# Fused attention, gated MLP and product MLP on one core: a third buffer for the down products' high parts, prepared weights stored in 1 KB runs, and attention's PSUM banks closed apart from its stores

## The chip, the core and the metric

One core of a Trainium2 chip runs the whole program in one launch. The metric is the device time in microseconds (us), the median of several runs. TensorE is called PE here, VectorE DVE, ScalarE ACT, GpSimd POOL, and SyncE SP; all large transfers are issued in order from SP's queue. PE's clock has two levels, 2.4 and 1.2 GHz; a granted clock of 1.00 is the upper one.

## The reference

```python
def _attn_ref(q, k, v, tau):                 # q, k, v: (4, 8, 576, 64), tau: 0.02
    scores = scale * np.matmul(q, k.transpose(0, 1, 3, 2))
    thresh = np.max(scores, axis=-1, keepdims=True) - tau
    scores = np.where(scores >= thresh, scores, -1000000000.0)
    attn = np.exp(scores - np.max(scores, axis=-1, keepdims=True))
    attn = attn / (np.sum(attn, axis=-1, keepdims=True) + 1e-09)
    return np.matmul(attn, v).astype(np.float32)
def _moe_ref(x, w_in, w_out):                # x: (2304, 512), w_in: (512, 2048)
    h = x @ w_in
    return ((h * (1.0 / (1.0 + np.exp(-h)))) @ w_out).astype(np.float32)
def _moe2_ref(x, w_a, w_b, w_out):           # w_a, w_b: (512, 1536)
    return ((x @ w_a) * (x @ w_b) @ w_out).astype(np.float32)
```

The attention's output goes through the gated MLP (MLP1) and then through the product MLP (MLP2). The weights come as float64.

## The kernel before

**The work.** Attention runs as 144 tiles of 128 query rows by 576 keys. A tile is scored on PE (L512, L519), DVE takes the row minimum of the negated scores (L528), ACT the exponential (L542), DVE masks and sums (L545), PE transposes the result (L577) and multiplies it by v (L622). MLP1 takes the tokens in five blocks of 256 and two of 512 (blocks 5 and 6), each in 16 units of 128 hidden columns: ups into bank hb or hc (L747), tanh on ACT (L757), the gate on DVE (L760), a rounded high part on ACT (L763) and the low part on DVE (L766), then downs into the y banks (L807). Every product is three fp32r matmuls: high by low, high by high, low by high. MLP2 takes the tokens in three tiles of 768 and works by a Strassen-Winograd scheme with seven products (`ORDER`): per tile six groups of up products (L1120, 504 matmuls of 384 columns), then the down products (L1206, 252 matmuls). The sums between products are chain() on DVE and ACT (p1, u2, v, c22, c21, c12: L1048 to L1065).

**Weights.** MLP1's 32 chunks (split_weight) are rebuilt from float64 words during the early attention: low word and scaled high word on ACT, sign (L354) and join (L359) on DVE, the integer sum (total, L363) in four POOL pieces, high part on ACT (L367), low part on DVE (L371). Two raw buffers (wraw), one wc buffer. MLP2's 36 units (split_unit) are rebuilt during MLP1's last blocks and stored to DRAM (L905) in seven combinations each, from which MLP2 streams 512 KB tiles (L960).

**Order.** Nothing is placed by hand. Class Plan simulates the engines with costs in nanoseconds and issues the task of lowest rank that is ready; buffers are rings (RINGS), and a task that takes a ring's buffer waits for its release. The resulting order per engine is then fixed, since each engine issues in order; semaphores do the waiting at run time. The costs of a task, its rank and the ring sizes thus decide which instruction stands ahead of which. On SP, loads and stores share that one order.

**What the change touches.** RINGS: xr5 (raw x of blocks 5 and 6), tm (results of chain, 768 columns), zh (rounded high parts of the down products' inputs). split_weight and w1_chunk; load_x (low part of x, L719); split_unit and prepare_weights with dv() and ac(), the planner's costs; stream; the task `closed`, behind all of attention's tasks, at which the memory of attention is given back and the banks hc and y5 are opened:

```python
    closed = pl.add("none", 1, 0, close_attention, behind=[*att_tasks, *closed0])
    l = pl.add("DVE", dv(2 * n), rank, lo, [h], [lo_take])
    st = {x: dma(-1, P * 8 * TN, store(x, half, par), after=[s[t]])
```

The second line is the low part zl of a down product's input (its own ring has two buffers), the third the four stores of a down phase's results, which hold their tm buffers until they land.

## Time and profile before

| what | value |
|---|---|
| median of 3 runs | 1140.99 us (1138.83 to 1143.01) |
| profiled execution | 1144.45 us, span 1142.6 us |
| mean granted clock of PE | 0.987 |
| busy, share of the span | PE 97%, DVE 72%, ACT 50%, POOL 18% |
| attention with MLP1's first units | 0 to 490 us |
| rest of MLP1, preparation of MLP2's weights | 490 to 736 us |
| MLP2, three tiles | 736 to 1143 us |

The span is the time between the first and the last instruction on the core; the profiled execution's own time has 1.85 us around it. An engine's share is its busy time over the span, an average over stages that differ.

### The profile page before, as it was taken

The page shows a single profiled execution, that of the slowest core. Times are in us where ns is not written, and L with a number is a line of the kernel's source. Part 1 is how long each engine was busy: PE and PEld are TensorE (multiplying, and loading weights), DVE is VectorE, ACT ScalarE, POOL GpSimd, SP SyncE. Part 2 cuts the span into 40 slices and gives each one's busy share as a digit, 9 for nine tenths or more (in the row PEclk, how much of TensorE's full clock was granted, in tenths as well). Part 3 has the DMA queues.
Part 4 walks back from the last instruction along what each step waited for, and adds up shares of the span by engine and source line. Part 5 has one row for each costly group of instructions (what it writes and reads, how often), then busy time and mean ns, then how long its engine had stood idle before and what let it go on. Part 6 is the DMA issues. An engine that isn't in the chain of part 4 may idle for free.

```text
span 1142.6 us, 19524 instructions
## 1 busy us (share of the span) xinstructions
PE 1105.2 (97%) x7097; PEld 985.2 (86%) x7097; DVE 822.8 (72%) x1702; ACT 574.1 (50%) x1012; POOL 201.9 (18%) x386
## 2 busy tenths in 40 slices
PE   8889998999999999999999899999989999999998
PEld 6457766898889989999888688899989999999998
DVE  8888887777777777739888789566764668546664
ACT  7777776666766676646665645311332113411133
POOL 2445444333423343122000200000000000000000
PEclk9989999999999999999999899999999999999999
DMA  6554454222332232139999979988879878887882
GB/s 198 184 166 155 147 156 122 97 80 87 89 98 75 76 104 75 38 123 273 287 269 284 276 219 327 323 247 255 256 261 304 249 255 246 269 281 253 248 252 75
DMA packets 147231, 222.27 MB, mean 195 GB/s; under 512 B 8112, under 2 KB 107584, under 8 KB 147136
## 3 DMA queue, kind: packets, MB, share of 16 engines
q1 hardware_dynamic: 146992, 221.03, 62.4%
q8 instruction: 56, 0.92, 0.3%
q14 instruction: 39, 0.32, 0.1%
q10 hardware_dynamic: 144, 0.00, 0.0%
HBM read 173.74 MB, written 47.26 MB: 193 GB/s over the span
## 4 chain that ended last, share of the span: by engine, by line
PE 81%; DMA 7%; DVE 5%; ACT 4%; issue 2%; POOL 1%; SPq 0%; POOLq 0%; DVEq 0%; ACTq 0%
PE pr L1120 23%; PE hb L747 11%; PE pr L1206 9%; PE sb L807 8%; PE av L622 6%; PE tp L577 5%; PE hc L747 5%; PE sa L512 4%; PE yc L807 2%; PE yd L807 2%; PE ye L807 2%; PE yf L807 2%; DMA wraw<-w_out 1%; DMA xi<-r_d 1%; DMA wraw<-w_in 1%
## 5 line engine op out<-in xcount | busy, mean ns | idle before, releaser
L1120 PE MATMUL pr<-w 128*128 128x384 f32 x1512 | 262.6, 334 | 0.0
L1120 PEld LDWEIGHTS pr<-w 128*128 128x128 f32 x1512 | 262.2, 188 | 0.1
L747 PE MATMUL hb<-xh,w 128*128 128x256 f32 (+1 forms) x704 | 156.9, 312 | 2.6 <-DVE th L760 1.9
L528 DVE TENSOR_SCALAR_CACHE_REDUCE t<-sa,nscale 128x576 f32<-128x576 f32 x128 | 103.5, 809 | 53.0 <-PE sa L512 45.5
L1206 PE MATMUL pr<-zh,w 128*128 128x384 f32 x504 | 129.2, 338 | 0.0
L545 DVE SCALAR_TENSOR_TENSOR e<-t,thr,e 128x576 f32<-128x576 f32 x128 | 112.0, 876 | 23.8 <-ACT e L542 22.3
L747 PEld LDWEIGHTS hb<-xh,w 128*128 128x128 f32 x704 | 113.9, 191 | 12.8 <-DVE th L760 3.1
L577 PE MATMUL tp<-ident,e 128*128 128x128 f32 x706 | 107.5, 280 | 12.0 <-DVE e L545 7.5
L577 PEld LDWEIGHTS tp<-ident,e 128*128 128x128 f32 x706 | 79.7, 142 | 36.4 <-issue 14.2
L542 ACT ACTIVATE e<-t,min 128x576 f32<-128x576 f32 x128 | 99.8, 781 | 19.7 <-DVE t L528 18.7
L747 PE MATMUL hb<-xl,w 128*128 128x256 f32 (+1 forms) x352 | 107.1, 304 | 0.7 <-POOL xl L719 0.7
L807 PE MATMUL sb<-gh,w 128*128 128x256 f32 (+1 forms) x576 | 98.1, 301 | 0.0
L1206 PEld LDWEIGHTS pr<-zh,w 128*128 128x128 f32 x504 | 91.9, 190 | 0.0
L1206 PE MATMUL pr<-zl,w 128*128 128x384 f32 x252 | 86.4, 343 | 4.9 <-DVE zl L975 4.8
L807 PEld LDWEIGHTS sb<-gh,w 128*128 128x128 f32 x576 | 80.1, 190 | 6.3 <-issue 3.3
L971 ACT CAST zh<-z 128x768 fp32r<-128x768 f32 x45 | 37.5, 833 | 84.1 <-PE pr L1206 58.4
L363 POOL TENSOR_TENSOR wt<-wc,wt 128x128 uint32<-128x128 uint32 x128 | 62.3, 517 | 77.3 <-DVE wc L359 48.4
L1132 ACT COPY yo<-pr 128x384 f32<-128x384 f32 x18 | 8.7, 481 | 123.7 <-PE pr L1120 123.7
L747 PEld LDWEIGHTS hb<-xl,w 128*128 128x128 f32 x352 | 67.1, 191 | 3.7 <-POOL xl L719 0.9
L512 PE MATMUL sa<-sp 128*128 128x288 f32 (+1 forms) x400 | 69.9, 300 | 0.0
L584 ACT COPY pb<-tp 128x512 f32<-128x512 f32 (+2 forms) x128 | 60.3, 493 | 17.7 <-PE tp L577 17.5
L719 POOL TENSOR_TENSOR xl<-xr,xh 128x128 fp32r<-128x128 f32 x72 | 39.3, 574 | 165.5 <-ACT xh L716 160.9
(140 smaller groups left out, 2016.6 us busy)
## 6 DMA issues: line engine op xcount, KB each, us to landing
w<-wab_d SPq DMA_DIRECT2D x126, 512.0 KB
w<-wo_d SPq DMA_DIRECT2D x63, 512.0 KB
wab_d<-uw SPq DMA_DIRECT2D x18, 896.0 KB
qk<-qk SPq DMA_DIRECT2D x20, 576.0 KB
wo_d<-uw SPq DMA_DIRECT2D x10, 896.0 KB
wraw<-w_in SPq DMA_DIRECT2D x16, 512.0 KB
wraw<-w_out SPq DMA_DIRECT2D x16, 512.0 KB
v<-v SPq DMA_DIRECT2D x20, 320.0 KB
```

The source lines that it names most:

```text
L363: nc.gpsimd.tensor_tensor(out=s["t"][:, o], in0=s["c"][:, o].bitcast(U32), in1=s["t"][:, o], op=ALU.add)
L512: nc.tensor.matmul(s["s"][:r + m, j, :NH], lhsT=hd["t"][:, 0, c - r:c + m], rhs=hd["t"][:, k, j * NH:(j + 1) * NH], start=(k == 1), stop=( ...
L528: nc.vector.tensor_scalar(out=s["t"], in0=s["s"][:, :, :NH], scalar1=nscale, scalar2=None, op0=ALU.mult, op1=ALU.min, accum_out=s["min"])
L542: nc.scalar.activation(out=s["e"], in_=s["t"], func=AF.Exp, scale=-1.0, bias=s["min"])
L545: nc.vector.scalar_tensor_tensor(out=s["e"], in0=s["s"][:, :, :NH] if early else s["t"], scalar=s["thr"], in1=s["e"], op0=ALU.is_ge if ear ...
L577: nc.tensor.transpose(t["tp"][:, j * P:(j + 1) * P], e["e"][:, o:o + P], ident)
L584: nc.scalar.copy(out=dst(s["p"]), in_=t["tp"][:, :m * P] if m < 4 else t["tp"].rearrange("p (k q) -> p k q", k=4))
L622: nc.tensor.matmul(s["av"][h * D:(h + 1) * D, :nq], lhsT=v["v"][:, h, k], rhs=s["p"][:, k, h * nq:(h + 1) * nq], start=(k == 0), stop=(k = ...
L747: nc.tensor.matmul(s["h"], lhsT=w[:, a, o:o + P], rhs=xx, start=(c == 0 and k == 0), stop=(c == NC - 1 and k == 2))
L807: nc.tensor.matmul(ys[j][e // per][:, e % per * tn:(e % per + 1) * tn], lhsT=w[:, a, e * P:(e + 1) * P], rhs=gs[j, f][g], start=(f == 0 an ...
L1120: nc.tensor.matmul(bank[:, m, :TN], lhsT=w["w"][:, a, (2 * m + k) * P:(2 * m + k + 1) * P], rhs=y[i][x][:, k, :TN], start=(i in (1, 6, 5) ...
L1206: nc.tensor.matmul(bank[:, c, :TN], lhsT=w["w"][:, a, (2 * e + c) * P:(2 * e + c + 1) * P], rhs=z[x][:, e], start=(i in (1, 6, 5) and sl = ...
```

## The change

xr5 and zh get a third buffer, tm loses one of five. The integer sum of the MLP1 chunks of the last two column groups (16 of 32) goes from POOL to DVE. The low part of block 6's x goes from POOL to DVE. Prepared weights are laid out so that a unit's high and low rows lie side by side, in SBUF and in DRAM, and its store writes runs of 1 KB where it wrote 512 bytes. Planner costs change: fixed parts of dv() and ac(), the sign step, more bytes and slack for the prepared weights' transfers. Attention's PSUM pools get their own stack, closed by a task (closed_p) that stands behind attention's PE, ACT and DVE tasks only; closed still stands behind its stores.

```diff
-    wab_d = dram.tile([NG, 7, P, 2, 4, P], F32, name="wab_d")
+    wab_d = dram.tile([NG, 7, P, 4, 2, P], F32, name="wab_d")
...
-    p1, p1x, px, att, psb = (ExitStack() for _ in range(5))
-    RINGS = dict(qk=2, sp=2, v=1, t=2, e=4, pa=1, pb=1, sa=1, sb=1, tp=2, hb=1, hc=1, yc=1, yd=1, ye=1, yf=1, xr5=2, x5=5, g5=2, th5=1, av=1, x=1, xi=1, rs=1,
+    p1, p1x, px, att, attp, psb = (ExitStack() for _ in range(6))
+    RINGS = dict(qk=2, sp=2, v=1, t=2, e=4, pa=1, pb=1, sa=1, sb=1, tp=2, hb=1, hc=1, yc=1, yd=1, ye=1, yf=1, xr5=3, x5=5, g5=2, th5=1, av=1, x=1, xi=1, rs=1,
...
-                 ur=2, us=2, uw=2, vr=2, vs=2, vw=1, yr=1, pr=4, tm=5, a11=2, zh=2, zl=2, **{f"z{k}": 3 for k in range(5)})
+                 ur=2, us=2, uw=2, vr=2, vs=2, vw=1, yr=1, pr=4, tm=4, a11=2, zh=3, zl=2, **{f"z{k}": 3 for k in range(5)})
...
-    ps_s = pool(att, "ps_s", 1, space=PSUM)
-    ps_t = pool(att, "ps_t", 2, space=PSUM)
-    ps_av = pool(att, "ps_av", 1, space=PSUM)
+    ps_s = pool(attp, "ps_s", 1, space=PSUM)
+    ps_t = pool(attp, "ps_t", 2, space=PSUM)
+    ps_av = pool(attp, "ps_av", 1, space=PSUM)
...
-    def split_weight(key, src, rank, dst, after=(), lo_engine="Pool", scale_engine="DVE", most=512):
+    def split_weight(key, src, rank, dst, after=(), lo_engine="Pool", scale_engine="DVE", most=512, total_engine="Pool"):
...
-            nc.gpsimd.tensor_tensor(out=s["t"][:, o], in0=s["c"][:, o].bitcast(U32), in1=s["t"][:, o], op=ALU.add)
+            eng = nc.gpsimd if total_engine == "Pool" else nc.vector
+            eng.tensor_tensor(out=s["t"][:, o], in0=s["c"][:, o].bitcast(U32), in1=s["t"][:, o], op=ALU.add)
...
-        ts = on_pool(512, rank, total, [j, l], most)
+        if total_engine == "Pool":
+            ts = on_pool(512, rank, total, [j, l], most)
+        else:
+            ts = [pl.add("DVE", dve_ns(512), rank, lambda: total(slice(0, 512)), [j, l], port=True)]
...
-        engines = dict(scale_engine=SCALE_ON[i % len(SCALE_ON)], lo_engine=LO_ON[i % len(LO_ON)], most=PIECE)
+        engines = dict(scale_engine=SCALE_ON[i % len(SCALE_ON)], lo_engine=LO_ON[i % len(LO_ON)], most=PIECE, total_engine=("Pool", "DVE")[j > 1])
...
-            def lo(o):
-                nc.gpsimd.tensor_tensor(out=s["l", c][:, o], in0=s["r", c][:, o], in1=s["h", c][:, o].bitcast(F32), op=ALU.subtract)
+            def lo(o, eng=nc.gpsimd):
+                eng.tensor_tensor(out=s["l", c][:, o], in0=s["r", c][:, o], in1=s["h", c][:, o].bitcast(F32), op=ALU.subtract)
...
-            l = on_pool(tn, R_AUX, lo, [h], PIECE)[-1]
+            if j == len(BLOCKS) - 1:
+                l = pl.add("DVE", dve_ns(tn), R_AUX, lambda: lo(slice(0, tn), nc.vector), [h], port=True)
+            else:
+                l = on_pool(tn, R_AUX, lo, [h], PIECE)[-1]
...
-                       behind=[up_last[0], *([closed] if c == 0 and bank == "hc" else [])])
+                       behind=[up_last[0], *([closed_p] if c == 0 and bank == "hc" else [])])
...
-                       banks if f == 0 and k0 == 0 else [], behind=[down_last[0], *([closed] if j >= 4 and f == 0 else [])])
+                       banks if f == 0 and k0 == 0 else [], behind=[down_last[0], *([closed_p] if j >= 4 and f == 0 else [])])
...
-        return int(n / 0.96 + 170)
+        return int(n / 0.96 + 67)
...
-        return int(n / 1.2 + 180)
+        return int(n / 1.2 + 93)
...
-            s["w"] = new("w", [P, 2, 7, P], F32R)
-            nc.scalar.copy(out=s["w"][:, 0], in_=s["a"][:, 1:])
+            s["w"] = new("w", [P, 7, 2, P], F32R)
+            nc.scalar.copy(out=s["w"][:, :, 0], in_=s["a"][:, 1:])
...
-            eng.tensor_tensor(out=s["w"][:, 1], in0=s["a"][:, 1:], in1=s["w"][:, 0].bitcast(F32), op=ALU.subtract)
+            eng.tensor_tensor(out=s["w"][:, :, 1], in0=s["a"][:, 1:], in1=s["w"][:, :, 0].bitcast(F32), op=ALU.subtract)
...
-            nc.sync.dma_start(out=dst.rearrange("i p l n -> p l i n"), in_=s["w"].bitcast(F32))
...
-        a = dma(rank, P * 4096, load, n=2, take=[lane + "r"], behind=behind)
+            nc.sync.dma_start(out=dst.rearrange("i p l n -> p i l n"), in_=s["w"].bitcast(F32))
...
+        a = dma(rank, P * 4096 * 6 // 5, load, n=2, slack=SLACK, take=[lane + "r"], behind=behind)
...
-        h = pl.add("DVE", 600, rank, sign, [a, c], port=True)
+        h = pl.add("DVE", 335, rank, sign, [a, c], port=True)
...
-        st = dma(rank, P * 7168, store, after=[o], slack=SLACK)
+        st = dma(rank, P * 7168 * 6 // 5, store, after=[o], slack=SLACK)
...
-                    units.append(((m, k, g), [r[h, k, :, :, g * P:(g + 1) * P] for h in range(2)], wab_d[g, :, :, :, 2 * m + k]))
+                    units.append(((m, k, g), [r[h, k, :, :, g * P:(g + 1) * P] for h in range(2)], wab_d[g, :, :, 2 * m + k]))
...
-                units.append((("o", g, c), [r[h, g, :, :, c * P:(c + 1) * P] for h in range(2)], wo_d[:, g // 2, :, :, g % 2, c]))
+                units.append((("o", g, c), [r[h, g, :, :, c * P:(c + 1) * P] for h in range(2)], wo_d[:, g // 2, :, g % 2, c]))
...
-            s["w"] = pools["ws"].tile([P, 2, 512], F32R, name="w")
-            nc.sync.dma_start(out=s["w"].bitcast(F32), in_=src)
+            s["w"] = pools["ws"].tile([P, 2, 512], F32R, name="w").rearrange("p a (q l n) -> p (a q) l n", q=2, l=2)
+            nc.sync.dma_start(out=s["w"].rearrange("p q l n -> p q (l n)").bitcast(F32), in_=src)
...
-            w = stream(wab_d[g, PART[i]].rearrange("p l q n -> p l (q n)"),
+            w = stream(wab_d[g, PART[i]].rearrange("p q l n -> p q (l n)"),
...
-                            nc.tensor.matmul(bank[:, m, :TN], lhsT=w["w"][:, a, (2 * m + k) * P:(2 * m + k + 1) * P],
+                            nc.tensor.matmul(bank[:, m, :TN], lhsT=w["w"][:, 2 * m + k, a],
...
-                w = stream(wo_d[PART[i], sl].rearrange("p l g c n -> p l (g c n)"),
+                w = stream(wo_d[PART[i], sl].rearrange("p g c l n -> p (g c) (l n)"),
...
-                                nc.tensor.matmul(bank[:, c, :TN], lhsT=w["w"][:, a, (2 * e + c) * P:(2 * e + c + 1) * P],
+                                nc.tensor.matmul(bank[:, c, :TN], lhsT=w["w"][:, 2 * e + c, a],
...
+    def close_banks():
+        attp.close()
...
+    closed_p = pl.add("none", 1, 0, close_banks, behind=[t for t in att_tasks if t["engine"] in ("PE", "ACT", "DVE")])
...
```

Which instruction stands where is the planner's result. Three places of it follow; the numbers behind a tile's name are running numbers of the plan.

ACT, transition from block 5 to block 6 of MLP1, before. th and gh are a unit's tanh and high part (block 6's first unit is th_8561), xh the high part of a quarter of x, yo the staging tile of a y bank on its way to DRAM (ye and sb are such banks), us, vs, uw and vw belong to MLP2's weights:

```order
L757 ACTIVATE th_8465<-hc 128x512
L763 CAST gh_8466<-th_8465 128x512
L898 CAST uw<-us 128x896
L870 ACTIVATE us<-ur 128x512
L716 CAST xh_8523<-xr_8477 128x512
L873 ACTIVATE us<-ur 128x512
L827 ACTIVATE yo<-ye 128x512
L827 ACTIVATE yo<-sb 128x512
L898 CAST vw<-vs 128x896
L757 ACTIVATE th_8561<-hb 128x512
L870 ACTIVATE vs<-vr 128x512
L873 ACTIVATE vs<-vr 128x512
L763 CAST gh_8562<-th_8561 128x512
```

ACT at the same place in the changed kernel (block 6's first unit is th_8463):

```order
L877 ACTIVATE us<-ur 128x512
L720 CAST xh_8406<-xr_7184 128x512
L764 ACTIVATE th_8413<-hc 128x512
L880 ACTIVATE us<-ur 128x512
L877 ACTIVATE vs<-vr 128x512
L770 CAST gh_8414<-th_8413 128x512
...
L764 ACTIVATE th_8463<-hb 128x512
L877 ACTIVATE us<-ur 128x512
L880 ACTIVATE us<-ur 128x512
L770 CAST gh_8464<-th_8463 128x512
L834 ACTIVATE yo<-ye 128x512
L905 CAST uw<-us 128x7x128
L764 ACTIVATE th_8522<-hc 128x512
L770 CAST gh_8523<-th_8522 128x512
...
L764 ACTIVATE th_8571<-hb 128x512
L834 ACTIVATE yo<-sb 128x512
```

The last quarter's xh stands ahead of block 5's last tanh, the first tanh of block 6 ahead of both yo, and yo<-sb, which stood ahead of the first tanh, stands two units behind it.

DVE, first down phase of MLP2, before. zl is the low part of a down product's input, w and z are those inputs, yr and yt the attention's output as read back and converted:

```order
L975 TENSOR_TENSOR w<-yt_9117,w 128x2x384
L1163 TENSOR_TENSOR z_10118<-z_9920,z_9957 128x768
L975 TENSOR_TENSOR zl<-z_9939,zh 128x768
L1166 TENSOR_TENSOR z_9920<-z_9920,z_9939 128x768
L975 TENSOR_TENSOR zl<-w,zh 128x768
L1170 TENSOR_TENSOR w<-z_9957,z_9920 128x2x384
L975 TENSOR_TENSOR w<-yr,w 128x2x384
L1174 TENSOR_TENSOR w<-z_9922,w 128x2x384
L975 TENSOR_TENSOR zl<-w,zh 128x768 x2
...
L1007 TENSOR_TENSOR yt_10167<-yr 128x768
L1007 TENSOR_TENSOR yt_10168<-yr,yt_10167 128x768
L975 TENSOR_TENSOR zl<-z_9920,zh 128x768
L1007 TENSOR_TENSOR yr<-yr 128x2x384
```

DVE there in the changed kernel:

```order
L982 TENSOR_TENSOR w<-yt_9191,w 128x2x384
L1145 TENSOR_TENSOR z_9868<-tm 128x384
L1072 TENSOR_TENSOR tm<-pr_9909,tm 128x768
L982 TENSOR_TENSOR w<-yr,w 128x2x384
L1145 TENSOR_TENSOR z_9886<-tm 128x384
L982 TENSOR_TENSOR zl<-z_9868,zh 128x768
L1170 TENSOR_TENSOR z_10057<-z_9845,z_9886 128x768
L982 TENSOR_TENSOR zl<-w,zh 128x768
...
L1014 TENSOR_TENSOR yt_10052<-yr 128x768
L982 TENSOR_TENSOR zl<-z_9845,zh 128x768
L1014 TENSOR_TENSOR yt_10053<-yr,yt_10052 128x768
L982 TENSOR_TENSOR zl<-z_9531,zh 128x768
```

The w<-yr,w of the first group, which reads yr last ahead of the next loads, stood behind two zl, two z sums and a w, and now stands ahead of them; one zl now stands between the first yt and the second, and one between that and the sum in place.

DVE, attention's late weight chunks, before: sign (L354), join (L359), low part (L371), with the sum on POOL:

```order
L371 TENSOR_TENSOR w<-wt,w 128x512
L354 TENSOR_SCALAR wraw<-wraw 128x512
L766 TENSOR_TENSOR gl<-th,gh 128x256
L359 SCALAR_TENSOR_TENSOR wc<-wc,wraw 128x512
L528 TENSOR_SCALAR t,min<-sa,nscale 128x576
L536 TENSOR_SCALAR thr<-min,tadd 128x1
L528 TENSOR_SCALAR t,min<-sa,nscale 128x576
L371 TENSOR_TENSOR w<-wt,w 128x512
L354 TENSOR_SCALAR wraw<-wraw 128x512
L545 SCALAR_TENSOR_TENSOR e,sum<-t,thr,e 128x576
L359 SCALAR_TENSOR_TENSOR wc<-wc,wraw 128x512
```

DVE there in the changed kernel:

```order
L364 ISA wt<-wc,wt 128x1024
L532 TENSOR_SCALAR t,min<-sa,nscale 128x576
L372 TENSOR_TENSOR w<-wt,w 128x512
L767 SCALAR_TENSOR_TENSOR th<-th,hb 128x256
L354 TENSOR_SCALAR wraw<-wraw 128x512
L540 TENSOR_SCALAR thr<-min,tadd 128x1
L359 SCALAR_TENSOR_TENSOR wc<-wc,wraw 128x512
L773 TENSOR_TENSOR gl<-th,gh 128x256
L364 ISA wt<-wc,wt 128x1024
L549 SCALAR_TENSOR_TENSOR e,sum<-t,thr,e 128x576
L532 TENSOR_SCALAR t,min<-sa,nscale 128x576
L372 TENSOR_TENSOR w<-wt,w 128x512
```

The sum (L364) now stands on DVE behind the join of its chunk, and the low part (L372) two instructions behind it.

## Rows read from the trace of the kernel before

**Rows 1.** Page, engines' busy time, share of the span, instructions.

```profile
PE 1105.2 (97%) x7097; PEld 985.2 (86%) x7097; DVE 822.8 (72%) x1702; ACT 574.1 (50%) x1012; POOL 201.9 (18%) x386
```

**Rows 2.** Windows: us; PE, PEld, DVE, ACT, POOL busy; PE clock; DMA share; GB/s.

```profile
105.00:204.00 99.00, 92.54 (x667) 70.23 (x664) 80.73 (x207) 72.10 (x145) 45.70 (x89) 0.98 0.48 141
490.00:642.00 152.00, 151.35 (x893) 133.60 (x890) 119.68 (x241) 91.30 (x160) 18.46 (x33) 1.00 0.86 254
642.00:660.00 18.00, 13.70 (x50) 10.69 (x49) 13.25 (x26) 9.31 (x15) 1.14 (x3) 0.81 0.96 286
823.40:873.00 49.60, 46.08 (x254) 44.80 (x253) 31.02 (x35) 18.04 (x22) 0.00 (x0) 0.97 0.83 277
844.00:873.00 29.00, 28.55 (x155) 28.23 (x156) 15.09 (x17) 9.86 (x12) 0.00 (x0) 0.94 0.79 260
1006.00:1093.40 87.40, 87.40 (x506) 87.40 (x506) 50.51 (x64) 9.38 (x14) 0.00 (x0) 1.00 0.82 258
```

**Rows 3.** Timelines of ACT, PE (start, duration, idle before), then chain, 642:660.

```profile
646.30 0.60 ACT L827 ACTIVATE yo<-sb 128x512 f32<-128x512 f32 x1 [3.17 <-DMA yT_d<-yo]
...
651.00 1.22 PE L807 MATMUL yc<-gh,w 128*128 128x512 f32 x2 [4.30 <-ACT gh L763]
...
644.97 3.94 DMA yT_d<-yo
656.37 2.76 PE hb L747 x12
```

**Rows 4.** Instruction groups: count, then sum and mean ns; L371's and 876 from 105:201.

```profile
L545 DVE SCALAR_TENSOR_TENSOR e<-t,thr,e 128x576 f32<-128x576 f32 x25 | 21.9, 876 | 6.0 <-ACT e L542 5.1
L371 DVE TENSOR_TENSOR w<-wt,w 128x512 fp32r<-128x512 f32 x15 | 10.5, 697 | 1.5 <-ACT w L367 1.2
...
L545 DVE SCALAR_TENSOR_TENSOR e<-sa,thr,e 128x576 f32<-128x576 f32 x8 | 6.5, 816 | 0.9 <-ACT e L540 0.7
L887 DVE CUSTOM_DVE_ANT_0 us<-us 128x1024 uint16<-128x1024 uint16 x28 | 19.2, 684 | 0.0
L363 POOL TENSOR_TENSOR wt<-wc,wt 128x128 uint32<-128x128 uint32 x128 | 62.3, 517 | 77.3 <-DVE wc L359 48.4
```

**Rows 5.** Chain of waits, MLP2: start, duration, engine, tile, line.

```profile
736.03 87.38 PE pr L1120 x504
...
873.04 87.40 PE pr L1120 x504
...
1005.98 87.38 PE pr L1120 x504
...
1127.89 10.34 PE pr L1206 x58
```

**Rows 6.** Down phases: timelines of DVE and PE, then the chain's load.

```profile
1101.46 0.96 DVE L975 TENSOR_TENSOR zl<-w,zh 128x768 fp32r<-128x768 f32 x1 [1.05 <-ACT zh L971]
...
841.39 0.96 DVE L1007 TENSOR_TENSOR yt<-yr 128x768 f32<-128x768 f32 x1 [2.25 <-DMA yr<-yT_d]
844.27 0.69 PE L1206 MATMUL pr<-zl,w 128*128 128x384 f32 x1 [2.47 <-DVE zl L975]
...
832.72 8.58 DMA yr<-yT_d
```

**Rows 7.** Timelines of SP's queue and DVE where an up phase begins.

```profile
874.07 0.39 SPq L1216 DMA_DIRECT2D out<-tm  x1
1007.00 0.39 SPq L1216 DMA_DIRECT2D out<-tm  x1
...
877.32 0.96 DVE L1052 TENSOR_TENSOR tm<-pr,tm 128x768 f32<-128x768 f32 x1 [3.28 <-PE pr L1120]
```

**Rows 8.** Waits of PE: total us, times, longest us.

```profile
PE yc L807 <- ACT gh L763: 4.9, 2, 4.3
```

**Rows 9.** Chain of waits, attention's weight loads.

```profile
160.38 5.20 DMA wraw<-w_in
166.14 3.75 DMA wraw<-w_out
```

## The prediction

> **What bounds the kernel now.** I read the busy shares first, then the stages, then the waits inside the stages where TensorE loses time. TensorE (PE) is busy 97% of the span [rows 1], so only its idle and half-clock stretches can be won. The stretches by stage [rows 2] show where these lie: while MLP2's up products run (1006 to 1093.4) it is busy all the time at full clock, but from 105 to 204 us 92.54 of 99, from 642 to 660 us 13.70 of 18 at a clock of 0.81, and in the first down phase of MLP2 (823.4 to 873) 46.08 of 49.6 at 0.97. No other engine is the bound over the whole; VectorE (DVE) at 80.73 of 99 us is the closest one in the stretch 105 to 204. The DMA engines are 0.86 busy from 490 to 642 us, but PE is busy 151.35 of those 152 us, so their load costs nothing there by itself.
>
> **The change, part by part.** The sum is made against the profiled execution, 1144.45 us (span 1142.6), which is 3.5 us above the median of the three runs; the difference is then taken off the median, 1140.99.
>
> *Blocks 5 to 6 of MLP1.* In the rows [rows 3] a store of yT_d ends the wait of ACT's second eviction (yo<-sb, 3.17 us idle). The tanh of block 6's first unit stands behind it, and PE gets the first down product only at 651.00 after 4.30 us idle. Then the granted clock is at its lower level: the twelve downs take 5.37 us (651.00 to 656.37) where the next twelve matmuls of the same width take 2.76, so 2.6 us more. Loss 6.9 us. Two causes show in the order: block 6's last quarter of x is loaded late, because only two raw buffers exist (xr5), and yo<-sb stands ahead of th. With three raw buffers the four quarters are split early (for the last block their low parts are now four VectorE instructions of about 0.7 us, priced as L371 [rows 4], in a stretch where PE never waits for VectorE; without that cover they would cost 2.8 us), all of block 6's first ups come before block 5's last downs, and ACT issues yo<-ye, a cast, then th<-hc, with yo<-sb a unit later. PE has 12 ups (2.76 us) between the last down of block 5 and the first of block 6, and the gate of that one was started a unit before. Bounds 0 and -6.9; I take **-6.5**, since nothing that waits for a store is left ahead of th.
>
> *Down phases of MLP2, third zh buffer.* 504 up matmuls take 87.38 us [rows 5], so 252 down matmuls of the same width cost 43.7. From the end of one up phase to the start of the next (or to the last matmul's end, 1138.23) the down phases last 49.6 (823.42 to 873.04), 45.5 (960.45 to 1005.98) and 44.9 us: losses 5.9, 1.8 and 1.2, together 8.9. The pattern of the small ones [rows 6]: VectorE waits 1.05 us for ACT's zh, since ACT copies a finished product first (L1048) and only then casts the next zh; zl starts at 1101.46 and holds PE till about 1102.4. With a third buffer that cast stands ahead of the copy, since it needs no release any more, and zl has two steps' time. The large one: VectorE stands at yt<-yr until the load lands at 841.39 (issued 832.72, 8.58 us), a zl stands behind it, and PE idles 2.47 us and then runs part of 844 to 873 at half clock. Now both loads are issued earlier by one and two of SP's weight loads (2.08 us each, 87.38/42), the w that frees their buffer stands five VectorE instructions sooner, and one more zl stands ahead of the second yt. The landing then falls near 839, which leaves about 0.5 us. Bounds: 0 if zl's own two buffers set the pace, -8.9 if all goes; the steady steps in between show no idle with two zl buffers, so I take **-7.5**.
>
> *tm from five buffers to four.* This is what the third zh buffer is paid with, and it adds a wait. The four results of a down phase now hold all four buffers until their stores land. The next up phase's second sum (u2, L1052) takes the buffer of the result stored last. That store is issued at 874.07 and at 1007.00 [rows 7], 1.03 us after the first product of the next tile starts; u2 started at 877.32; PE's fourth product, which needs u2, starts three products later, 873.04 + 6.24 = 879.28. u2 (0.96 us) must therefore start by 878.25, so the store may take 4.2 us without loss. No row of before waits for such a store. The nearest are the yT_d store of 3.94 us (256 KB) and the yr load of 8.58 us (768 KB, beside the same weight stream): for 384 KB I take the middle, 6.3 us, a stall of 2.1 us at each of two transitions. Bounds 0 and 4.4 each, and half a clock window more (about 1.7 us, as after the 2.47 us idle) if it falls. **+4.5.** Behind the waiting u2 on VectorE stand only that tile's own sums.
>
> *Attention, 105 to 204 us.* For the last sixteen weight chunks the integer sum moves from GpSimd (POOL), four instructions of 517 ns, to VectorE, one; its twin there (L887) takes 684 ns [rows 4]. That puts 16 x 0.684 = 10.9 us on VectorE and takes 33 us off POOL. Each chunk's chain gets shorter by about 1.4 us plus a hand-over, and the planner now places the last chunk's low part after the 45th tile, not the 54th, and 21 MLP1 gates instead of 18 ahead of tile 55. Lower bound: PE's idle (6.5 us) and clock loss (2% of 99) all go, -8.4. Upper bound: VectorE stays 81.5% busy, so 10.9 us become 13.4 us of delay, less three units of MLP1 done meanwhile (72 matmuls of 256 columns, half the price of the 512-column ones, 8.3 us): +5.1. VectorE's masks with POOL beside them average 876 ns in this stretch [rows 4] against 816 in the first sixteen tiles, so some comes back. I take **-1**. The Trainium skill (GPSIMD Engine Reference, Specifications) says GpSimd shares its SBUF interfaces with VectorE and contends with instructions that have two SBUF inputs; the masks agree, and by it alone this term would be about -1.5 (25 masks by 60 ns).
>
> *Attention's banks closed apart from its stores.* hc and the y banks can be taken before the last xT_d store. The PE wait for gh outside the stall above is 4.9 - 4.3 = 0.6 us [rows 8]: **-0.5**, bounds 0 and -0.6.
>
> *1 KB runs.* The stores of 36 prepared units write 896 runs where they wrote 1792. PE waits for none of these stores (blocks 4 to 6 keep it at 151.35 of 152 us), and the weights lie as contiguous in SBUF as before for the matmuls: **0**, bounds 0 and nothing, and only if MLP2's first weight loads had to wait for the last store would they show. The planner's new cost figures (sign, fixed parts, stores by 6/5) are no work; what they do is the order, and that is counted in the terms above. The stretch with 512-byte runs moves 254 GB/s at 0.86, the one with long runs 258 at 0.82 [rows 2], so 295 against 315 GB/s per full share: 6% at most. The Trainium skill (DMA: Bandwidth & Descriptors, Specifications) has 512 B as the least transfer for full rate; by it the new runs gain nothing, and the trace nearly agrees.
>
> Sum: -6.5 - 7.5 + 4.5 - 1 - 0.5 = **-11.0**, so 1140.99 - 11.0 = **1130 us**.
>
> **The rivals.**
> *The out stores land in time* (15%): then no tm stall, -15.5, **1125.5**. For it: 3.94 us for a store under 0.96 DMA load. Against: weight loads queue ahead of it. The Trainium skill (DMA: Bandwidth & Descriptors, Anatomy of one DMA) gives a fixed 2 us plus bytes at 436 GB/s, an estimated 2.9 us for 384 KB, by which the store lands in time and there is no stall; the yr load's 8.58 us speaks against so short a landing.
> *The tm stall is large* (15%): 4.4 us twice and a clock drop of 1.7 each, 12.2 in place of 4.5: **1137.5**, -3.3, on the border.
> *zl, not zh, holds the down phases* (10%): the term -7.5 goes, **1137.5**. Against: steady steps don't idle.
> *Late weight chunks block VectorE* (10%): **slower, 1146**. A load of a raw chunk takes 3.75 to 5.20 us on the chain [rows 9]; with two ACT passes, sign and join a raw buffer is held about 7.5 us, and two buffers allow a chunk every 3.75 us. The new order asks for one about every 5. If queue waits make each chunk late by one microsecond, VectorE, which issues in order, holds the softmax behind it, 16 us in all. It decides from (11.0 + 3.4)/16 = 0.9 us per chunk. For it: VectorE is asked for more in a shorter stretch; against: the loop has 2.5 us to spare per two chunks.
> *The forecast*: 50%.
>
> **How the numbers follow.** About 0.3%, 3.4 us, is what a measurement can tell from no change. Faster: nearly all of the forecast (0.47), the first rival (0.15), two thirds of the border case (0.09), half of the zl case (0.05): 0.76. Slower: most of the late-chunk case and a remainder: 0.11. Same: 0.13. The range reaches from 1119 (all gains whole and attention at its lower bound, the tm stall small) to 1141 (both border cases, half of the attention's upper bound); outside lie the late chunks and a little below.
>
> **What would show it.** Right: no ACT wait on yT_d ahead of th near 640, PE without the 4.3 us gap and the clock whole there; down phases of 44 to 45 us each; L1052's successor waiting for an out<-tm store with a 2 us PE gap in the fourth product of the second and third tile. Wrong: VectorE idle on wt<-wraw or on the sum in 105 to 204 us with the 54th tile more than 9 us later; a first down phase that still waits for yr; a half-clock window behind the tm gap.

## The result and the profile after

The changed kernel took 1126.87 us (median of 4 runs, 1124.38 to 1128.0) beside 1140.46 for the kernel before (4 runs): ratio 0.9876, 95% interval 0.985 to 0.9902. The forecast was 1130 us in a range of 1119 to 1141. The profiled execution took 1128.0 us, span 1125.9, so 1.1 us above its median, where the one of before was about 4 above. The two spans differ by 16.7 us, the medians by 13.6.

The busy line of the page, to be set beside [rows 1]:

```profile
PE 1095.8 (97%) x7086; PEld 979.4 (87%) x7086; DVE 832.2 (74%) x1722; ACT 571.4 (51%) x1012; POOL 160.9 (14%) x306
```

GpSimd lost 41 us of work and VectorE gained 9. PE is busy 9.4 us less although it does the same products: half-clock matmuls count as busy. The stages, with the columns of [rows 2]:

```profile
105.00:204.00 99.00, 93.59 (x696) 71.22 (x694) 85.73 (x219) 71.21 (x143) 13.26 (x22) 1.00 0.45 138
204.00:490.00 286.00, 281.95 (x2280) 252.38 (x2280) 214.91 (x605) 192.77 (x373) 96.79 (x174) 0.99 0.26 82
490.00:642.00 152.00, 152.00 (x889) 133.31 (x886) 128.12 (x258) 91.20 (x162) 9.57 (x19) 1.00 0.80 261
642.00:660.00 18.00, 18.00 (x79) 14.59 (x78) 17.46 (x35) 10.79 (x17) 0.00 (x0) 1.00 0.89 297
815.70:859.40 43.70, 43.70 (x254) 43.70 (x254) 30.02 (x35) 18.04 (x22) 0.00 (x0) 1.00 0.91 317
```

From 642 to 660 us PE does 79 matmuls where it did 50, without a gap, and the first down phase of MLP2 (last line) is busy from end to end. The stretch from 105 to 204 gained 1 us of busy time and the whole clock, but 204 to 490, which was full before, has 4 us of idle time: in this execution.

The transition from block 5 to block 6 on PE and ACT (start, duration; a bracket would hold idle time), to be set beside [rows 3]:

```profile
644.18 0.63 PE L814 MATMUL yc<-gh,w 128*128 128x512 f32 x2
```
```profile
641.08 0.58 ACT L834 ACTIVATE yo<-ye 128x512 f32<-128x512 f32 x1
644.38 0.60 ACT L764 ACTIVATE th<-hc 128x512 f32<-128x512 f32 x1 [1.89 <-PE hc L754]
...
650.47 0.59 ACT L834 ACTIVATE yo<-sb 128x512 f32<-128x512 f32 x1
```

The first down product of block 6 has no idle time ahead of it (it had 4.30 us). ACT waits for PE now and not for a store, and yo<-sb runs nine microseconds after yo<-ye. The chain of waits, last part, beside [rows 5]:

```profile
719.94 2.80 PE hc L754 x12
725.54 2.09 PE pr L1127 x12
730.39 85.30 PE pr L1127 x492
815.69 43.68 PE pr L1213 x252
859.37 87.38 PE pr L1127 x504
946.75 43.68 PE pr L1213 x252
990.43 87.38 PE pr L1127 x504
1077.81 43.69 PE pr L1213 x252
```

All three down phases are one unbroken row of 252 matmuls in 43.7 us, the floor that the prediction had worked out. So MLP2 lost nothing any more: 5.9 + 1.8 + 1.2 = 8.9 us are gone. The first line shows something else: twelve 512-column matmuls of block 6 take 2.80 us, where [rows 3] has 2.76 after the gap. This spacing of the matmuls is called their rhythm below.

The four tm buffers, on VectorE at the start of the second tile (beside [rows 7]); the store before it was issued at 860.39:

```profile
863.64 0.96 DVE L1059 TENSOR_TENSOR tm<-pr,tm 128x768 f32<-128x768 f32 x1 [3.28 <-DMA out<-tm]
```

The second sum is put down to a store, but it starts just after its product ended (859.37 + 2 x 2.08 = 863.53), as it did before with five buffers (873.04 + 4.16 = 877.20, start 877.32 in [rows 7]), and PE runs on: the chain has one row of 504 matmuls there.

Where the 16.7 us between the two spans went: up to block 6's first down product 651.00 - 644.18 = 6.8, of it the gap 4.3 and 2.5 from attention and blocks 0 to 4; from there to MLP2 85.0 against 84.1 (728.31, which is 815.69 - 87.38, less 644.18), 0.9; the down phases 8.9.

### The profile page after: what moved, and what is told of

The parts are those of the page before. It is cut to its first block, busy times and chain, and to the rows that moved or that the text cites. A ratio compares the mean times of both kernels' runs of the same rounds, so it can differ in the third digit from the quotient of the medians.

```text
span 1125.9 us, 19426 instructions
## 1 busy us (share of the span) xinstructions
PE 1095.8 (97%) x7086; PEld 979.4 (87%) x7086; DVE 832.2 (74%) x1722; ACT 571.4 (51%) x1012; POOL 160.9 (14%) x306
## 4 chain that ended last, share of the span: by engine, by line
PE 62%; DMA 0%; ACT 0%; DVE 0%; POOL 0%; issue 0%; ACTq 0%
PE pr L1127 23%; PE pr L1213 12%; PE hb L754 7%; PE hc L754 5%; PE sb L814 4%; PE yd L814 2%; PE yc L814 2%; PE yf L814 2%; PE ye L814 2%; PE av L626 1%; PE tp L581 1%; PE sa L516 1%; DMA xT_d<-x 0%; DVE tm L1072 0%; PE av L631 0%; ACT pb L588 0%
## 5 line engine op out<-in xcount | busy, mean ns | idle before, releaser
L661 POOL TENSOR_TENSOR x<-x,xi 128x128 f32<-128x128 f32 (+2 forms) x80 | 41.6, 544 | 190.3 <-DMA xi<-r_d 88.9
L447 POOL TENSOR_TENSOR sp<-qk,sp 64x115 fp32r<-64x115 f32 (+1 forms) x100 | 58.0, 611 | 52.2 <-issue 36.6
```

The lines of the kernel that those rows point to most:

```text
L447: nc.gpsimd.tensor_tensor(out=s["t"][D:, 0, o], in0=s["r"][D:, o], in1=s["t"][D:, 0, o].bitcast(F32), op=ALU.subtract)
L661: nc.gpsimd.tensor_tensor(out=s["x"][:, o], in0=s["x"][:, o], in1=s["i"][:, o], op=ALU.mult)
```

## The experiments

Each expectation was on record before its run. Runs 1 to 4, runs 5 to 8 and runs 9 to 12 each shared a chip and its runs of the kernel before, so their medians compare within a group (before: 1137.78, 1143.95 and 1137.13 us).

### 1. The third zh buffer, paid for with one tm buffer

```diff
-    ... pr=4, tm=5, a11=2, zh=2, zl=2 ...
+    ... pr=4, tm=4, a11=2, zh=3, zl=2 ...
```

> The kernel before with one part of the change: three zh buffers, four tm buffers. Theory A (the third zh buffer alone shortens the down phases, and four tm buffers cost PE nothing because the next tile's first sums take the buffers of the results that were stored first): all three down phases at 43.7 to 44.5 us where they took 49.6, 45.5 and 44.9, PE's 4.3 us gap at block 6 still there, so 8 to 9 us faster than before, 1131 to 1133 us. Rival B (the first phase's wait for yr went because the planner's new costs moved the loads): the small losses of 1.8 and 1.2 us go, the wait of 2.5 us and its clock loss stay, 3 us faster, about 1138. Rival C (four tm buffers hold up the second sum of a tile once the order is this one): PE gaps of about 2 us in the fourth product of tiles two and three, 1135 to 1137.

Measured: 1133.59 us, ratio 0.9957 (0.994 to 0.9975). Its chain of waits in MLP2:

```profile
734.61 87.40 PE pr L1120 x504
...
866.91 87.40 PE pr L1120 x504
...
958.89 39.45 PE pr L1206 x226
998.33 87.38 PE pr L1120 x504
1085.71 43.69 PE pr L1206 x252
```

The down phases take 44.9 (734.61 + 87.40 = 822.01 to 866.91), 44.0 and 43.7 us: 7.3 of the 8.9 us come with these two ring sizes, the yr wait's clock loss among them, and run 6 shows that the tm buffer has no part in it. Rivals B and C fall by these rows. The median gained only 4.2 us, between the 8 to 9 of theory A and the 3 of rival B; the interval of the ratio ends at 6.8 us, so why the medians show less than the phases is open.

The load of yr itself did not move forward here. The second one is issued 15.3 us behind the end of the up phase (837.30 - 822.01), where before it was 9.3 (832.72 - 823.42), and still PE's longest wait for a zl in this phase is 0.25 us:

```profile
837.30 0.44 SPq L995 DMA_DIRECT2D yr<-yT_d  x1
```
```profile
850.35 0.44 PE L1206 MATMUL pr<-zl,w 128*128 128x384 f32 x1 [0.25 <-DVE zl L975]
```

### 2. The third raw buffer, with block 6's low part on VectorE

```diff
-    ... xr5=2 ...
+    ... xr5=3 ...
...
-            l = on_pool(tn, R_AUX, lo, [h], PIECE)[-1]
+            if j == len(BLOCKS) - 1:
+                l = pl.add("DVE", dve_ns(tn), R_AUX, lambda: lo(slice(0, tn), nc.vector), [h], port=True)
+            else:
+                l = on_pool(tn, R_AUX, lo, [h], PIECE)[-1]
```

> The kernel before with one part: three xr5 buffers, and the low part of block 6's x on VectorE. Theory A (the third raw buffer ends the wait at block 6): the 4.3 us gap and the half-clock stretch of 2.6 us go, of which 1.5 us come back if the 512-column matmuls stay at 233 ns to the end of MLP1 as they do in the changed kernel (before they take 229 from block 6 on): 4.5 to 6.9 us faster, 1134 to 1136 us, the down phases of MLP2 unchanged at 49.6, 45.5, 44.9. Rival (the gap is owed to the order of the evictions that the planner's costs and the banks' closing set): the gap stays within 1 us, 1139 to 1141.

Measured: 1133.65 us, ratio 0.9977 (0.996 to 0.9993), so the median is 4.1 us lower and the ratio gives 2.6. PE's timeline at block 6 and a late row of the chain:

```profile
643.17 0.40 PE L750 MATMUL hc<-xl,w 128*128 128x512 f32 x1
643.40 0.63 PE L810 MATMUL yc<-gh,w 128*128 128x512 f32 x2
```
```profile
719.16 2.80 PE hc L750 x12
```

The gap is gone with the raw buffer and the low part on VectorE, without the new costs and the banks; the two were not tried apart. The rhythm of 2.80 us per twelve matmuls then lasts to the end of MLP1, and takes 1.5 us of the gain back. Against the expectation, the first down phase did not stay at 49.6 us but took 47.1 (814.94 to 862.00), so the profile shows more gain than the time does.

### 3. The sum on VectorE alone

```diff
-            nc.gpsimd.tensor_tensor(out=s["t"][:, o], in0=s["c"][:, o].bitcast(U32), in1=s["t"][:, o], op=ALU.add)
+            eng = nc.gpsimd if total_engine == "Pool" else nc.vector
+            eng.tensor_tensor(out=s["t"][:, o], in0=s["c"][:, o].bitcast(U32), in1=s["t"][:, o], op=ALU.add)
...
+            ts = [pl.add("DVE", dve_ns(512), rank, lambda: total(slice(0, 512)), [j, l], port=True)]
...
```

> The kernel before with one part: the integer sum of the last 16 weight chunks on VectorE. Theory A (the attention's balance is near zero): PE idle from 105 to 204 us 1 to 2 us less than 6.5 and the clock there whole, part of it lost again after 204 us; sum -3 to +1, 1138 to 1142 us. Rival B (VectorE is the closest engine there and each sum delays it): 10.9 us of work more on VectorE cost 3 to 5 us, 1144 to 1146. Rival C (the shorter chain per chunk is worth the whole idle time): 6 us faster, 1134.

Measured: 1131.2 us, ratio 0.9945 (0.9926 to 0.9964), the 6 us of rival C. In this order PE waits only 1.13 us at block 6, and the rhythm changes early:

```profile
554.08 2.80 PE hb L751 x12
...
559.64 2.75 PE hc L751 x12
...
714.96 2.75 PE hc L751 x12
```

The 2.75 us last from 560 us to the end of MLP1; the kernel before has them from 656 us on, so block 5 gains 0.05 us on each of some 30 groups of twelve, 1.5 us. The shorter gap (3.2 us) and the half clock that does not follow it (2.6) make 5.8 more. Together that is the whole 6.3 us of the ratio and more, so by the times little is left for attention: rival C had the size, and the larger part of its cause lies in block 5 and behind it. The profiles say otherwise of attention: block 5 starts at 544.1 us here, at 549.9 in the profile of before, and at 546.7 in run 6, whose instructions stand in the order of before. So what the sum does there is not shown.

### 4. The planner's new costs alone

```diff
-        return int(n / 0.96 + 170)
+        return int(n / 0.96 + 67)
...
-        return int(n / 1.2 + 180)
+        return int(n / 1.2 + 93)
...
-        h = pl.add("DVE", 600, rank, sign, [a, c], port=True)
+        h = pl.add("DVE", 335, rank, sign, [a, c], port=True)
...
-        st = dma(rank, P * 7168, store, after=[o], slack=SLACK)
+        st = dma(rank, P * 7168 * 6 // 5, store, after=[o], slack=SLACK)
```

> The kernel before with the planner's new costs for the prepared weights alone (dv, ac, sign, transfers by 6/5 with slack). Theory A (they only move instructions, and nothing of what was lost is owed to them): within 1.5 us of before, 1139 to 1142 us, the gap at block 6 between 3 and 5 us. Rival B (they are what takes the evictions' place ahead of the tanh away): the gap at block 6 goes, 5 to 6 us faster, 1135. Rival C (sparser planning than the chip takes delays the stores of the prepared weights): PE waits for weights at the start of MLP2, 2 us or more slower.

Measured: 1139.43 us, ratio 1.002 (1.0004 to 1.0037): a little slower, just outside what theory A allowed, and not where rival C looked. PE's timeline, the rows with waits and two at the lower clock (0.84 from 642 to 660 us):

```profile
640.01 0.74 PE L747 MATMUL hb<-xh,w 128*128 128x512 f32 x2 [3.44 <-ACT xh L716]
...
642.87 0.79 PE L747 MATMUL hb<-xl,w 128*128 128x512 f32 x1 [2.12 <-POOL xl L719]
643.46 1.05 PE L747 MATMUL hc<-xh,w 128*128 128x512 f32 x2
644.31 0.63 PE L747 MATMUL hc<-xl,w 128*128 128x512 f32 x1
...
649.77 0.72 PE L807 MATMUL yc<-gh,w 128*128 128x512 f32 x2 [1.46 <-ACT gh L763]
```

With these costs and only two raw buffers, block 6 waits for its own x, first the high part, then GpSimd's low part: 7.0 us in three pieces, the last for the gate's high part, where theory A had 3 to 5 us. So the costs are worth nothing by themselves, with two raw buffers and the low part on GpSimd.

### 5 and 10. Breaking the rhythm

```diff
-                    nc.tensor.matmul(s["h"], lhsT=w[:, a, o:o + P], rhs=xx,
-                                     start=(c == 0 and k == 0), stop=(c == NC - 1 and k == 2))
+                    for lo, hi in ((0, 384), (384, 512)) if big and f == 0 and c == 0 and k == 1 else ((0, tn),):
+                        nc.tensor.matmul(s["h"][:, lo:hi], lhsT=w[:, a, o:o + P], rhs=xx[:, lo:hi],
+                                         start=(c == 0 and k == 0), stop=(c == NC - 1 and k == 2))
```

Run 10 has f == 2 in place of f == 0.

> The changed kernel with one matmul of 512 columns in the first unit of block 5, and one in the first unit of block 6, split into 384 and 128 columns. In the profiles so far the 512-column matmuls run every 233.3 ns from block 5 on until PE's weight loads are late once (by 35 ns in the run with the sum on VectorE, by the 4.3 us gap before), or until matmuls of 384 columns come in between (the changed kernel at 725 us), and every 229 ns after that. Theory A (a fixed rhythm of weight loads and matmuls, which any odd piece breaks for good): 229 ns from the split on, 740 matmuls by 4 ns, 3 us faster than the changed kernel. Rival B (the rhythm depends on the memory traffic of the weights' preparation, not on the matmuls): still 233 ns, no difference, and block 6's rhythm changes at another time.

> The changed kernel with the same split into 384 and 128 columns, now in the third unit of blocks 5 and 6. In the run with the split in the first unit, block 5's split broke the rhythm of 233 ns, but sixteen matmuls of 256 columns that followed brought it back; block 6's broke it for good. Theory A (only what follows decides): 229 ns from the third unit of block 5 to the end of MLP1, so MLP2 starts 1.5 us earlier after block 5's start than with the first split and 3 us earlier than in the changed kernel: block 5's start to MLP2's 179 us where the changed kernel has 182. Rival (it is the place, not the piece): 233 ns until block 6's split, 180.5 us.

Measured: run 5 1123.14 us, ratio 0.9834 (0.9807 to 0.9861); run 10 1118.56 us, ratio 0.9827 (0.9807 to 0.9847), beside 0.9875 (0.9855 to 0.9895) and 1123.57 us for the changed kernel in run 10's group. Run 5's group holds no run of the changed kernel; run 8 there, without a split, has the same ratio, so by time run 5 shows no gain, and what follows of it is read from the profile. Groups of twelve ups on the chain, first of run 5, then of run 10:

```profile
547.63 2.80 PE hc L755 x12
...
626.03 2.80 PE hc L755 x12
637.21 2.75 PE hc L755 x12
...
708.62 2.75 PE hb L755 x12
```
```profile
545.82 2.80 PE hc L755 x12
557.00 2.75 PE hc L755 x12
...
710.89 2.75 PE hc L755 x12
```

In run 5 the split in block 6 (631.7 us) changes the rhythm for good. The split in block 5 (542.0 us) is followed by one more 512-column matmul and then by 256-column matmuls of block 4, twelve and not sixteen before the next of 512 columns; that one and all behind it are 233 ns apart. Run 10's split comes after all of those and holds. From block 5's first matmul to MLP2 (counted from 87.4 us ahead of its first down product) run 10 takes 179.0 us, run 5 180.5 and the changed kernel in run 9 182.1, as theory A of run 10 had it; the other 1.3 us between the profiles of runs 9 and 10 lie ahead of block 5. **Run 10 beats both kernels**, by 0.5% the changed one, of which the profiles give about 0.3% to the rhythm. Rival B of run 5 (memory traffic) falls, since only PE's own instructions were touched.

### 6. Four tm buffers alone

```diff
-    ... pr=4, tm=5, a11=2, zh=2 ...
+    ... pr=4, tm=4, a11=2, zh=2 ...
```

> The kernel before with four tm buffers in place of five, nothing else. Theory A (the result that is stored last is not the one whose buffer the next tile's second sum takes; that sum takes the buffer of the result stored second, which landed long before): no PE gap in the first 10 us of tiles two and three, time within 0.2% of before. Rival (my prediction's term: the second sum waits for the last store): PE gaps of 2 us each in the fourth product of tiles two and three, 4 us slower.

Measured: 1142.81 us, ratio 0.9996 (0.9978 to 1.0014). The order of every engine is that of before. VectorE's second sum and PE's stretches at the start of tiles two and three (columns as in [rows 2]):

```profile
874.57 0.96 DVE L1052 TENSOR_TENSOR tm<-pr,tm 128x768 f32<-128x768 f32 x1 [3.28 <-DMA out<-tm]
```
```profile
870.00:885.00 15.00, 15.00 (x88) 15.00 (x87) 6.55 (x9) 1.28 (x2) 0.00 (x0) 1.00 0.85 286
1003.00:1018.00 15.00, 15.00 (x89) 15.00 (x88) 6.62 (x9) 1.28 (x2) 0.00 (x0) 1.00 0.90 289
```

PE is busy all 15 us both times: the wait that the prediction added does not reach it. Since the order is that of before, this profile is also a second look at that kernel. Behind block 5's start it repeats the first within 0.4 us (186.4 us to MLP2 for 186.0, the wait at block 6 4.56 us for 4.30, down phases of 49.7, 45.5 and 44.9 us), but block 5 starts at 546.7 us where it started at 549.9.

### 7. The sum back on GpSimd

The reverse of run 3's diff, in the changed kernel.

> The changed kernel with the integer sum of all 32 weight chunks back on GpSimd. Theory A (the sum on VectorE is worth the 3.3 us that the stage from the start to block 5 is shorter, and part of the rhythm's 3 us came by accident in the run with the sum alone): 2 to 4 us slower than the changed kernel, all of it ahead of block 5. Rival B (it is worth the 6 us measured alone): 6 us slower. Rival C (nothing, the two stages' profiles differ by chance): same within 1 us.

Measured: 1127.84 us, ratio 0.9862 (0.9833 to 0.9891). Beside runs 5 and 8 of its group, at 0.9834, that would be 3 us slower, but the intervals overlap. Masks in the stretch 105 to 201 us (count, then sum and mean ns), first of this run, then of the changed kernel's first profile:

```profile
L545 DVE SCALAR_TENSOR_TENSOR e<-t,thr,e 128x576 f32<-128x576 f32 x24 | 21.2, 883 | 5.8 <-ACT e L542 5.0
```
```profile
L549 DVE SCALAR_TENSOR_TENSOR e<-t,thr,e 128x576 f32<-128x576 f32 x23 | 19.0, 826 | 4.9 <-ACT e L546 4.8
...
L364 DVE CUSTOM_DVE_ANT_0 wt<-wc,wt 128x1024 uint16<-128x1024 uint16 x16 | 11.3, 709 | 0.0
```

A mask takes 50 to 57 ns less where GpSimd has less to do (13 us of busy time from 105 to 204 us, 46 before and 48 here), and the sixteen sums add 11.3 us to VectorE. By the profiles block 5 starts at 543.9 us here and at 541.3 in run 9, but less of block 4 is left behind that point here; MLP2's first down product starts at 812.12 us here, at 810.94 in run 9 and at 815.69 in the changed kernel's first profile. Attention's executions thus differ among themselves by more than the effect. Which of A and C holds is not settled.

### 8. Runs of 512 bytes

```diff
-    wab_d = dram.tile([NG, 7, P, 4, 2, P], F32, name="wab_d")
+    wab_d = dram.tile([NG, 7, P, 2, 4, P], F32, name="wab_d")
...
-            s["w"] = new("w", [P, 7, 2, P], F32R)
-            nc.scalar.copy(out=s["w"][:, :, 0], in_=s["a"][:, 1:])
+            s["w"] = new("w", [P, 2, 7, P], F32R)
+            nc.scalar.copy(out=s["w"][:, 0], in_=s["a"][:, 1:])
...
-            nc.sync.dma_start(out=dst.rearrange("i p l n -> p i l n"), in_=s["w"].bitcast(F32))
+            nc.sync.dma_start(out=dst.rearrange("i p l n -> p l i n"), in_=s["w"].bitcast(F32))
...
```

> The changed kernel with the old layout of the prepared weights: 512-byte runs in their stores, the order of all engines the same. Theory A (PE waits for none of these stores): the same time within 0.15%, a higher DMA share while the weights are prepared (0.92 to 0.94 where it is 0.89), MLP1's last block unchanged. Rival (longer transfers delay loads of x or of MLP2's first weights): PE gaps at block 6 or at MLP2's start, 2 us or more slower.

Measured: 1123.35 us, ratio 0.9834 (0.9804 to 0.9865), where the changed kernel has 0.9875 in another group: no sign that the 1 KB runs gain time. Every engine's order is that of the changed kernel. The same two stretches, first with 512-byte, then with 1 KB runs:

```profile
547.00:632.00 85.00, 85.00 (x366) 68.99 (x365) 78.06 (x151) 52.97 (x85) 0.00 (x0) 1.00 0.99 290
640.00:720.00 80.00, 80.00 (x344) 64.93 (x343) 65.76 (x112) 43.66 (x67) 0.00 (x0) 1.00 0.93 290
```
```profile
547.00:632.00 85.00, 85.00 (x377) 69.40 (x376) 78.39 (x152) 51.51 (x84) 0.00 (x0) 1.00 0.89 293
640.00:720.00 80.00, 80.00 (x344) 64.81 (x343) 66.94 (x118) 44.73 (x71) 0.00 (x0) 1.00 0.86 294
```

At about the same 290 GB/s the DMA engines are 0.99 busy against 0.89, and 0.93 against 0.86. PE is busy throughout in both, so the relief costs and gains nothing here; but with 512-byte runs nothing was left to spare.

### 9. The changed kernel again

> The changed kernel itself, beside the others on one chip. The order of its attention is that of two other runs whose blocks 0 to 4 ended at 540.8 and 541.7 us, while its first profile had 546.1. Theory A (the first profile had one more half-clock stretch by chance): block 5 starts between 540 and 546 us, the down phases last 43.7 us each, ratio to before between 0.983 and 0.989. Rival (the first profile is typical and the runs that differ from it are really faster): 546 us again, and a ratio of 0.987 or more beside 0.983 of its neighbours.

Measured: 1123.57 us, ratio 0.9875 (0.9855 to 0.9895). Block 5 starts at 541.3 us, 4.8 us earlier than in the first profile, with the same program; the down phases are 43.7 us each. Theory A's numbers hold, and the ratio is that of the first pair (0.9876). Its reason holds in part only: the mean granted clock is 0.995 for 0.994, worth about 1 us, and PE is busy 4.1 us longer up to 490 us (468.5 for 464.4). So these two profiles of attention differ by 4.8 us with the same instructions, and a difference of that size between two profiles shows nothing there.

### 11. The ring sizes without the rest

Run 1's and run 2's diffs together, in the kernel before.

> The kernel before with the three ring sizes and block 6's low part on VectorE alone: xr5=3, zh=3, tm=4; no new planner costs, sum on GpSimd, 512-byte runs, banks as before. Theory A (the rings carry the change): gap at block 6 gone, down phases 44.9, 44.0 and 43.7 as in the run with zh alone, so 7.3 + 4.5 = 12 us faster than before where the whole change has 14 to 18; attention as before. Rival (parts only pay together): less than 9 us.

Measured: 1127.04 us, ratio 0.9908 (0.9885 to 0.9931). The down phases take 44.5, 44.0 and 43.7 us and there is no gap at block 6: 10.1 of the 13.6 us between the group's medians come with the three ring sizes and the low part on VectorE. Theory A's 12 us was a little too much, and its rival, under 9, falls.

### 12. More sums on VectorE, with the split

```diff
-        engines = dict(... total_engine=("Pool", "DVE")[j > 1])
+        engines = dict(... total_engine=("Pool", "DVE")[j > 0])
```

and run 10's split.

> The changed kernel with the split in the third unit and with the integer sum on VectorE for 24 of the 32 chunks in place of 16. Theory A (eight more chunks have the shorter chain, and MLP1's first units are done earlier inside attention): block 5 starts 1 to 2 us earlier than in the run with the split alone. Rival (VectorE is the closest engine from 50 to 105 us, where these chunks lie, and 5.5 us more on it delays the softmax): 2 to 4 us later.

Measured: 1127.76 us (1119.23 to 1130.98), ratio 0.9896 (0.9863 to 0.9928). The stretches from 50 us on, first of run 10, then of this one:

```profile
50.00:105.00 55.00, 47.10 (x329) 33.33 (x329) 46.09 (x115) 41.93 (x83) 26.09 (x51) 0.94 0.55 169
...
204.00:490.00 286.00, 283.28 (x2300) 252.48 (x2300) 212.47 (x599) 191.64 (x371) 94.90 (x169) 1.00 0.25 80
```
```profile
50.00:105.00 55.00, 44.80 (x278) 30.59 (x277) 47.47 (x114) 38.92 (x76) 10.47 (x15) 0.84 0.53 162
...
204.00:490.00 286.00, 280.07 (x2244) 250.96 (x2244) 210.84 (x595) 188.13 (x364) 94.75 (x172) 0.98 0.25 81
```

In this execution the rival was right in sign and place and too small in size: from 50 to 105 us PE does 51 instructions fewer, at a clock of 0.84, and block 5 starts at 550.1 us, 10 us later than in run 10. Nearly all of that is clock: the mean granted clock is 0.988 for 0.996, and 0.8% of the span is 9 us. It does not come every time. Two of the six executions took 1119.23 and 1120.45 us, at 0.994 and 0.993, about as long as run 10; the other four took 1126.85 to 1130.98, at 0.987 to 0.990.

## Why the prediction was right, and where not

The forecast was 11.0 us; the spans show 16.7 and the medians 13.6. The direction and the range held because the two large terms, block 6 and the down phases, were right in the main. One term was wrong altogether (tm); without it the sum would have been 15.5, which is 1.9 us too much where 11.0 is 2.6 too little, so the closeness of the number is no proof of the parts. By terms:

- **Blocks 5 to 6**, -6.5 forecast: the gap (4.3 us) and the half clock (2.6 us) went as said, and run 2 ties the gap to the third raw buffer together with the low part on VectorE. But 1.5 us came back that the step had not: it took twelve matmuls at 2.76 us, the rhythm after the gap, as the price that would hold; without a gap the 2.80 us of block 5 goes on through the 360 matmuls from block 6's first down product to MLP2 (360 x 4 ns). So this part is worth about 5.4 us.
- **Down phases**, -7.5 forecast, -8.9 measured, the whole bound. Runs 1 and 6 give 7.3 to the zh ring, so the third rival (zl sets the pace) falls. The prediction had the large wait go in part because the loads of yr are issued earlier; in run 1 they are issued later than before and it is all but gone, so the earlier issue is not needed for it. Of the last 1.6 us, run 11 with both rings still lacks 1.2 (44.5, 44.0, 43.7). Runs 7 and 8, without the sum and without the layout, keep 43.7 in all three phases, so the costs or the banks remain, and these were not tried apart.
- **tm from five to four**, +4.5 forecast, 0 measured (run 6). This is the step that failed. It said that the second sum takes the buffer of the result stored last. The trace shows that it can't have waited for that store: the store issued at 860.39 lands by pieces until 865.27, and the sum starts at 863.64. The buffer that it takes was free in time; what takes the last one comes later, and PE waits for none of it. The size of the landing, 4.9 us, lay between the forecast's two nearest rows. With it the rest of the term, had it been right, would have been a stall of 0.7 us and not 2.1; and twice 2.1 is 4.2, so 0.3 of the 4.5 stand without a row. So the first rival's time, 1125.5, was nearest to the median, though not for the reason it named: no store had to land sooner. The second rival, a large stall, falls with it (its time is 1140.99 - 3.3 = 1137.7, not 1137.5). The Trainium skill (DMA: Bandwidth & Descriptors, Anatomy of one DMA) has a fixed 2 us plus bytes at 436 GB/s, an estimated 2.9 us here, as a fit for transfers that GpSimd issues. This store was issued by SP beside the stream of weight loads and took 4.9, so the prediction's use of that figure did not hold here.
- **Attention and banks**, -1.5 forecast, 2.5 us earlier in the first pair of profiles, which is less than the 3.2 by which two profiles of the order of before differ at block 5's start (run 6) and the 4.8 of the changed kernel (run 9). The runs don't settle it: run 7 against its neighbours 3 us, with overlapping intervals, and by profile between the two of the changed kernel. No run tried the banks alone. The direction of the masks was right: 876 ns before, 826 after, 883 with the sum back on GpSimd. The Trainium skill (GPSIMD Engine Reference, Specifications) has the two engines share their SBUF interfaces, and these three rows agree.
- **1 KB runs and planner costs**, 0 forecast. Run 8 shows the first; for the second run 4 shows +2 us, the costs alone with two raw buffers, and no run takes them out of the changed kernel. The 6% that the prediction read for short runs from two different stages is 10% when the same stage is compared. The Trainium skill (DMA: Bandwidth & Descriptors, Specifications) names 512 B as the least transfer for full rate; here 512-byte runs need a tenth more DMA time than 1 KB runs for the same bytes, so the measurement speaks against it.

The rival on the slower side (late chunks holding VectorE) did not come with 16 chunks; in run 12, with 24, four of six executions lost 8 us and more beside run 10's median, in the profiled one most of it to the clock, though which wait brings the clock down was not taken apart.

What stays open: whether the sum on VectorE gains anything by itself, what the banks and the new costs are worth in the changed kernel, and why the times of runs 1 and 2 show less than their profiles.

## What to carry to other kernels

Before charging a smaller ring with a stall, follow which buffer the next taker gets: only the release of that one matters, not the last. A buffer that lets a cast stand ahead of an eviction can be worth more than its memory, and here three ring sizes, with one low part on another engine, carried 10 of 13.6 us. Compare stages between profiles only when they vary less than the effect; attention here varied by 5 us with an unchanged program. Look at every execution's time and clock before taking one profile as typical (run 12).

## What the runs showed of the hardware

512-column fp32r matmuls ran in one of two rhythms at the same granted clock of 1.00: 233 ns each (twelve in 2.80 us) or 229 ns (2.75). Three things were followed by a change from 233 to 229 that stayed to the end of MLP1: one weight load that started 0.27 us behind the one before in place of 0.23 (run 3, at 556.52 us), a gap of 4 us (before and runs 1 and 6), and a split piece of 384 and 128 columns (run 10, and block 6 in run 5). In run 5's block 5, where one more matmul and then twelve of 256 columns came behind the split, the next ones of 512 columns were 233 ns apart. Why there are two rhythms is not shown. At the lower clock two of the same matmuls take 0.85 us (643.46 to 644.31 in run 4's timeline), so 425 ns each, less than twice either. A kernel that never lets PE wait can therefore be slower per matmul than one with a hiccup: with one split matmul in block 5 and one in block 6 this stretch was 3.1 us shorter.
